# Attention, gated MLP and feed-forward block in one kernel: head 0 loaded ahead and written by the engines, slack for loads on ScalarE, and the output weights converted beside the MoE block of batch 0

## The chip, the cores and the metric

The kernel runs on one core of one Trainium2 chip. The time is the device time of one execution in microseconds; runs of the kernel before gave 665.03, 667.38 and 668.51 us, median 667.38. The engines are PE (TensorE), DVE (VectorE), ACT (ScalarE), POOL (GpSimd) and SP (SyncE, which here only issues DMAs; ACT issues some too).

## The reference

Three stages run one after the other, on 2 batches of 768 positions:

```
# 1 attention: 8 heads of 64; 6 hash bits per row from the sign of q.proj and k.proj
mask   = bucket(q) == bucket(k)
scores = where(mask, q @ k.T / 8, -1e9)
x      = softmax(scores) @ v                       # heads side by side: (2, 768, 512)
# 2 "MoE" block, a gated MLP
u, v   = split(relu(x @ w_in))                     # w_in 512 x 1024, so 512 and 512
gated  = u * (w_spatial @ layernorm(v) + b_spatial)
x      = gated @ w_out                             # 512 x 512
# 3 feed-forward
out    = x + relu(layernorm(x) * g_ln @ w_ch1) @ w_ch2    # 512 -> 2048 -> 512
```

The weights of stages 2 and 3 arrive as float64, seen as pairs of 32-bit words; q, k, v and the result are float32.

## The kernel before, in words

**Precision.** PE multiplies in a reduced float32 form (F32R). To keep accuracy, each operand is kept as a high part (rounded to F32R) and a low part (the rest), and a product is three passes: high by high, high by low, low by high.

**Attention.** Work goes by (batch, head, group g of 384 queries, tile j of 128 queries): 96 tiles, six to a head. `scores` (line 787) makes a 128x768 tile `sc` in PSUM from `qs` and `ks`: a first matmul over 128 rows (high and low parts of one head stacked) and a second over 76 rows, which adds the high parts and 12 indicator rows. The indicator rows make the mask: `mismatch` (line 700) multiplies the raw q and k of a pair of heads by `sides` (signed copies of the projections), and a comparison on DVE makes the tile `m` of them, with rows that add a huge number wherever a bit differs. `masked_max` (line 799) reads `sc` on DVE into `x` and finds the row maximum; `exps` (816) is ACT's exponential; `transposes` (822) turns `x` on PE into `pt`, which ACT and DVE copy to `e`; after six tiles `weighted` (839) multiplies by v into `po`.

**Head pairs.** `pair_load` (670) loads q and k of two heads into 128 partitions (64 each), `pair_split` (682) makes high and low parts, and `passes_of` (723) gathers them with DMAs on SP into `ks` (per head) and `qs` (per group). For the very first head there is a shorter way: `first_load` (748) also loads head 0's k, and its q of group 0, into partitions 64 to 127 of a tile `dup`, and `first_parts` (754) has the engines write `ks` and the `qs` of group 0 directly, the indicator rows too. Group 1 of head 0, and head 1, still come through `pair_split` and SP's DMAs. While the first data arrive, PE runs 16 + 8 transposes of an identity into a tile `warm`.

**Weights.** Each weight of stage 2 is converted once from float64 words, in 4 pieces of 128x512 per matrix: ACT issues the load (`stage_f64`, 561), ACT and DVE work on the words (`words_f64`, 567), POOL joins them (`join_f64`), ACT and POOL split them into high and low. `conversions` (973) lists w_out, then the v half, then the u half of w_in; `CONV_AT` gives the attention tile at which each piece begins (5, 9, ... 57) and `CONV_D` the delays of its four steps. A finished matrix is written whole to DRAM (`kept`, 963), and loaded back by `reload` (994) when a batch needs it. w_out is collected in the tile that later holds the normalized v (`vn`).

**Stages 2 and 3.** `moe1(0)` begins at attention tile 60 and runs interleaved with tiles 60 to 95; `moe1(1)` runs with the first matmuls of stage 3 (`up`, `down`), whose weights `w1` and `w2` are converted in pieces like those above (`f_w`, `f64c_w`, `w1t`, `w2t`), in buffers (`conv1`, two of them) that open when attention ends.

**What sets the order.** No engine's order is the program's. Each call makes a Job; `run` (296) is a list scheduler with modelled durations, which picks on every engine the ready job that is due first; `latest` (397) works back from the end for due times; twelve rounds alternate, the best is kept, and `issue` (472) emits each engine's instructions in that order. A job isn't planned more than `EARLY` = 20 us ahead of its due time, nor more than 60 jobs ahead of PE. `plan.behind` names a job that the next jobs are planned after; it makes no semaphore. On the chip an engine runs its instructions strictly in that order, and waits where data are late; ACT's DMA issues stand in the same order as its arithmetic.

Every instruction of the program is recorded at line 494, where `issue` emits it, so the rows are told apart by tiles.

Of the kernel before, what the change touches and what calls it, by code (L numbers as in the profile page):

```python
# [18 lines left out]
P = 128  # L19
# [150 lines left out]
class Plan:  # L170
# [12 lines left out]
    NEXT = 0.03  # L183
    LAND = {"load": 2.0, "move": 1.5, "store": 1.5}
    RATE = {"load": 300e3, "move": 195e3, "store": 200e3}

    def __init__(self, tc):
        self.tc, self.jobs, self.pools, self.part, self.behind = tc, [], [], 0, None
        for name, key in (("tensor", "PE"), ("vector", "DVE"), ("scalar", "ACT"), ("gpsimd", "POOL"), ("sync", "SP")):
            setattr(self, name, Engine(self, key))  # L190

    def add(self, engine, op, args, kw):
        writes = [kw["out"] if "out" in kw else args[0]]
        rest = [*(args if "out" in kw else args[1:]), *(x for k, x in kw.items() if k not in ("out", "accum_out"))]
        if "accum_out" in kw:
            writes.append(kw["accum_out"])
        reads = [x for x in rest if isinstance(x, View)]
        views = [(x, True) for x in writes if isinstance(x, View)] + [(x, False) for x in reads]
        prev = self.jobs[-1] if self.jobs else None
        if (  # L200
            engine == "PE"
            and prev is not None
            and prev.engine == "PE"
            and prev.part == self.part
            and not prev.closed
            and prev.out is writes[0].base
            and prev.kind == (op, cells(writes[0]), writes[0].rows)
            and len(prev.calls) < (12 if cells(writes[0]) == 384 and op == "matmul" and reads[0].dtype == F32 else self.RUN)
        ):
            job = prev  # L210
        else:
            job = Job(len(self.jobs), engine, self.part)
            self.jobs.append(job)
            if engine == "PE":
                job.out, job.kind = writes[0].base, (op, cells(writes[0]), writes[0].rows)
        if self.behind:
# [15 lines left out]
    def cost(self, engine, op, writes, reads, kw, job):  # L232
# [12 lines left out]
        if engine == "PE":  # L245
            if op == "transpose":
                return (0.109 if isinstance(reads[0], View) else 0.213), 0.165
# [48 lines left out]
    def run(self, late=None):  # L296
# [20 lines left out]
        def opened(j):  # L317
# [182 lines left out]
def attn_moe_kernel(ctx: ExitStack, tc: tile.TileContext, qT, kT, v, proj, w_in, w_spT, b_sp, w_out, g_ln, w1, w2, out):  # L500
# [20 lines left out]
    CONV_AT = (5, 9, 14, 19, 24, 29, 34, 39, 44, 49, 53, 57)  # L521
# [9 lines left out]
    WARM2 = 8  # L531
# [68 lines left out]
    nc.sync.dma_start(out=pj[0:D], in_=proj)  # L600
# [69 lines left out]
    def pair_load(b, r, first=False, which=(("k", kT), ("q", qT))):  # L670

        pr = pairs.setdefault((b, r), {})
        for nm, src in which:
            pr[nm] = ap.tile([P, 2, S], F32R, tag=nm + "2", name=f"{nm}2_{b}_{r}", bufs=1 if nm == "k" else 2)
            if first:
                raw = ap.tile([P, S], F32, tag="x", name=f"{nm}_raw", bufs=XB)
            else:
                raw = pr[nm][:, LOW[nm]].bitcast(F32)
            nc.sync.dma_start(out=raw, in_=src[b, 2 * r : 2 * r + 2].rearrange("h d s -> (h d) s"))
            pr[nm, "raw"] = raw  # L680

    def pair_split(b, r, first=False):

        for nm in "kq":
# [4 lines left out]
            if first:  # L689
                nc.scalar.activation(hi, raw, AF.Copy, scale=scale)  # L690
# [9 lines left out]
    def mismatch(b, r):  # L700


        m = ap.tile([P, GW], F32R, tag="m", name=f"m_{b}_{r}", bufs=2)
        pm = ps_b.tile([P, GW], F32, tag="b", name=f"pm_{b}_{r}")

        for n, (nm, g) in enumerate((("k", 0), ("k", 1), ("q", 0), ("q", 1))):
            raw = pairs[b, r][nm, "raw"]
            nc.tensor.matmul(
                pm[n * QUAD : (n + 1) * QUAD], side[nm], raw[:, g * GW : (g + 1) * GW], start=True, stop=True
            )  # L710
        nc.vector.tensor_scalar(m, pm, above, worth, op0=ALU.is_gt, op1=ALU.mult)
# [36 lines left out]
    def first_load():  # L748
        dup = ap.tile([P, NKT, GW], F32, tag="e", name="dup", bufs=EB)
        nc.sync.dma_start(out=dup[D:P, 0:2], in_=kT[0, 0].rearrange("d (a s) -> d a s", a=2))  # L750
        nc.sync.dma_start(out=dup[D:P, 2], in_=qT[0, 0, :, 0:GW])
        return dup

    def first_parts(dup):
# [3 lines left out]
        qs = ap.tile([P, 2, GW], F32R, tag="qs", name="qs_0_0_0", bufs=QB)  # L758
# [3 lines left out]
        two = pr["q", "raw"][0:D, 0:GW].rearrange("d (o s) -> d o s", o=1).to_broadcast([D, 2, GW])  # L762
        nc.scalar.activation(qs[0:D], two, AF.Copy, scale=-SCALE)
        nc.scalar.activation(qs[D:P, 0], dup[D:P, 2], AF.Copy, scale=-SCALE)
        nc.vector.scalar_tensor_tensor(
            qs[D:P, 0], dup[D:P, 2], -SCALE, qs[D:P, 0].bitcast(F32), op0=ALU.mult, op1=ALU.subtract
        )
        heads[0, 0], groups[0, 0, 0] = {"ks": ks}, {"qs": qs}
        for n, to in enumerate((ks[D:MR, 1, 0:GW], ks[D:MR, 1, GW:S], qs[D:MR, 1])):
            rows = pr["m"][n * QUAD : n * QUAD + NM].bitcast(F32)  # L770
            if n == 1:
                nc.scalar.activation(to, rows, AF.Copy)
            else:
                nc.vector.tensor_copy(to, rows)
# [24 lines left out]
    def masked_max(b, h, g, j):  # L799
# [14 lines left out]
        t["x"], t["nb"] = x, nb  # L814
# [61 lines left out]
    def attn_step(i):  # L876
# [19 lines left out]
        if 0 < n < NT and order[n][3] == 0:  # L896
            group_prep(*order[n][:3])
# [44 lines left out]
    def converted(src, dst, nm, after=None):  # L942
# [12 lines left out]
        def finish():  # L955
            to = dst()
            split_f64(to[:, 0], to[:, 1], d["f"])
            if after:
                after(to)

        return stage, words, join, finish

    def kept(key, shape, to):
        w_split[key] = dram.tile(shape, F32, tag=f"ws_{key}", name=f"ws_{key}")
        nc.scalar.dma_start(out=w_split[key], in_=to.bitcast(F32))
# [7 lines left out]
    def conversions():  # L973

        res = []
        for key, src, at in (("out", w_out, 0), ("v", w_in, HF), ("u", w_in, 0)):
            for k in range(KFT):

                def dst(key=key, k=k):
                    if k == 0:  # L980
                        if key == "out":
                            wp[key] = mp.tile([P, 2, NKT, HF], F32R, tag="vn", name="w_out", bufs=1)
                        else:
                            wp[key] = moe_tile(key, 0)
                    return wp[key][:, :, k : k + 1]

                def after(to, key=key):
                    kept(key, [P, 2, KFT, HF], wp.pop(key)[:, :, :KFT])

                src_k = src[:, k : k + 1, at : at + HF]  # L990
                res.append(converted(src_k, dst, f"{key}_{k}", after if k == KFT - 1 else None))
# [161 lines left out]
    for i in range(-1 - QA, NT + PO + 3):  # L1153
# [212 lines left out]
```

## Time and profile before

| | |
|---|---|
| median of 3 runs | 667.38 us (665.03 to 668.51) |
| the profiled execution | 669.14 us |
| its span, first to last instruction | 666.8 us |
| mean granted PE clock over the span | 0.992 |
| busy: PE / DVE / ACT / POOL | 651.5 / 430.3 / 302.1 / 198.3 us |
| DMA, mean | 126 GB/s |

The span is what the trace covers; the time of an execution holds some 2 us more. "Busy" of PE is modelled: matmuls are pipelined, so back to back they count as busy without a gap. The clock is a share of full speed: 1.00 is 2.4 GHz, 0.50 is 1.2 GHz. In a timeline, the bracket behind an instruction tells how long its engine was idle before it and what ended that; xN is how many like instructions were merged. "PE", "ACT" and so on are the engines' own work; "SPq" and "ACTq" are DMA issues.

### The profile page before, as it was taken

What the parts mean: (1) busy time and instruction counts of PE and PEld (TensorE: products, weight loads), DVE (VectorE), ACT (ScalarE), POOL (GpSimd) and SP (SyncE); (2) the same over time, 40 slices, a digit from 0 to 9 for tenths busy, and PEclk for the clock granted to TensorE, in tenths of its full rate; (3) what the DMA queues carried; (4) which work ended last, traced back from release to release, by engine and by line L of the source; (5) the groups of instructions that cost most, each with busy time, mean ns of one, the idle gap of its engine ahead of it and who ended that gap; (6) DMA issues with size and microseconds to landing.
All of it is one profiled execution on the core that took longest, in us unless ns stands there. A gap on an engine that the chain in (4) does not pass through costs nothing.

```text
span 666.8 us, 9374 instructions
## 1 busy us (share of the span) xinstructions
PE 651.5 (98%) x3376; PEld 510.2 (77%) x3376; DVE 430.3 (65%) x804; ACT 302.1 (45%) x581; POOL 198.3 (30%) x184
## 2 busy tenths in 40 slices
PE   7999999989999999999899999999999999999997
PEld 5776767767777777877688888888888888888886
DVE  5699779998657544443899695788862358622122
ACT  5788877776556545433364343432321133311110
POOL 2234424446325311100324433054450044510000
PEclk8999999999999999999899999999999999999999
DMA  6776775755539442906343441722210222200031
GB/s 167 187 190 168 190 162 154 220 134 179 146 97 336 102 105 71 327 27 227 129 151 121 144 132 47 284 95 87 84 51 1 64 85 87 81 1 16 1 111 63
DMA packets 47413, 83.72 MB, mean 126 GB/s; under 512 B 5676, under 2 KB 32136, under 8 KB 46344
## 3 DMA queue, kind: packets, MB, share of 16 engines
q1 hardware_dynamic: 34104, 53.64, 28.3%
q10 hardware_dynamic: 13264, 29.50, 13.2%
q8 instruction: 27, 0.44, 0.3%
q14 instruction: 18, 0.15, 0.1%
HBM read 51.42 MB, written 12.58 MB: 96 GB/s over the span
## 4 chain that ended last, share of the span: by engine, by line
PE 87%; DVE 7%; DMA 3%; issue 1%; ACT 1%; POOL 0%; SPq 0%; ACTq 0%; DVEq 0%; POOLq 0%
PE pc L494 20%; PE acc L494 20%; PE pv L494 8%; PE po L494 8%; PE sc L494 8%; PE pg L494 8%; PE pt L494 7%; PE py L494 5%; DVE x L494 2%; DMA f_w<-in_w 1%; DVE f64c_u L494 1%; PE pm L494 1%; PE ptr_g L494 1%; PE px_c L494 1%; DMA qs<-m 1%
## 5 line engine op out<-in xcount | busy, mean ns | idle before, releaser
L494 PE MATMUL acc<-w2t,ch 128*128 128x512 f32 x576 | 141.8, 393 | 0.0
L494 PE MATMUL pc<-xh,w1t 128*128 128x512 f32 x576 | 141.8, 394 | 0.0
L494 PEld LDWEIGHTS pc<-xh,w1t 128*128 128x128 f32 x576 | 108.0, 188 | 24.7
L494 PEld LDWEIGHTS acc<-w2t,ch 128*128 128x128 f32 x576 | 108.0, 188 | 24.5
L494 ACT ACTIVATE x<-x,nb 128x768 f32<-128x768 f32 x96 | 89.7, 935 | 29.9 <-DVE x L494 27.9
L494 DVE TENSOR_SCALAR_CACHE_REDUCE x<-sc 128x768 f32<-128x768 f32 x96 | 90.9, 952 | 17.8 <-PE sc L494 12.0
L494 DVE SCALAR_TENSOR_TENSOR ch<-pc,ch 128x512 fp32r<-128x512 f32 x48 | 33.1, 690 | 106.5 <-ACT ch L494 106.4
L494 PE MATMUL sc<-ks,qs 128*128 128x512 f32 (+3 forms) x384 | 94.9, 367 | 6.9 <-DVE x L494 3.6
L494 ACT ACTIVATE ch<-pc 128x512 fp32r<-128x512 f32 x48 | 28.7, 598 | 146.1 <-PE pc L494 146.0
L494 PE MATMUL pt<-ident,x 128*128 128x128 f32 x576 | 82.6, 276 | 0.9 <-DVE m L494 0.6
L494 PEld LDWEIGHTS sc<-ks,qs 128*128 128x128 f32 (+1 forms) x384 | 64.3, 194 | 21.7 <-DVE x L494 5.7
L494 POOL TENSOR_TENSOR f64c_w<-f_w,f64c_w 128x512 f32<-128x512 f32 x32 | 44.6, 1395 | 114.6 <-DVE f64c_w L494 95.0
L494 PEld LDWEIGHTS pt<-ident,x 128*128 128x128 f32 x576 | 68.0, 142 | 13.3 <-ACT e L494 4.1
L494 ACT ACTIVATE e<-pt 128x384 f32<-128x384 f32 x120 | 55.8, 484 | 26.5 <-PE pt L494 25.8
L494 PE MATMUL po<-e,vv 128*64 128x384 f32 x384 | 65.5, 490 | 0.0
L494 DVE COPY e<-pt 128x384 f32<-128x384 f32 x72 | 39.6, 552 | 17.9 <-PE pt L494 17.6
L494 PEld LDWEIGHTS po<-e,vv 128*64 128x64 f32 x384 | 26.2, 137 | 31.3 <-issue 30.1
L494 PE MATMUL pg<-vn,w_sp 128*128 128x512 f32 x180 | 45.0, 399 | 0.0
L494 PE MATMUL pv<-w_u,act_x 128*128 128x512 f32 x144 | 36.3, 400 | 2.3 <-ACT xT L494 2.2
L494 PEld LDWEIGHTS pg<-vn,w_sp 128*128 128x128 f32 x180 | 33.0, 188 | 7.1
L494 DVE TENSOR_SCALAR f64c_w<-f64c_w 128x512 f32<-128x512 f32 x64 | 32.6, 511 | 7.2 <-ACT f64c_w L494 6.5
L494 PE MATMUL pv<-w_v,act_x 128*128 128x512 f32 x144 | 37.1, 406 | 0.0
(132 smaller groups left out, 777.5 us busy)
## 6 DMA issues: line engine op xcount, KB each, us to landing
f_w<-in_w ACTq DMA_DIRECT2D x32, 512.0 KB
ks<-k SPq DMA_DIRECT2D x45, 192.0 KB
qs<-q SPq DMA_DIRECT2D x31, 192.0 KB
wst_sp<-in_w_spT SPq DMA_DIRECT2D x12, 384.0 KB
w_out<-ws_out SPq DMA_DIRECT2D x2, 2048.0 KB
vv<-in_v SPq DMA_DIRECT2D x16, 192.0 KB
ot<-y_dram SPq DMA_DIRECT2D x12, 256.0 KB
qs<-q SPq DMA_DIRECT2D x31, 96.0 KB
```

The costliest lines, as they stand in the source:

```text
L494: getattr(getattr(nc, engine[j.engine]), op)(*map(live, args), **{k: live(x) for k, x in kw.items()})
```

## The change

Four edits. (1) At the start only head 0's halves of k and q are loaded first (64 partitions), then `dup`, now with both groups of q, then head 1's halves. A first `mismatch` works on rows 0 to 63 alone, followed by ten warm transposes (`WARM2`, 8 before); a second one on all rows follows later for head 1. `first_parts` writes the `qs` of both groups, and POOL copies one set of indicator rows. The low and high parts of the pair (`pair_split`) are planned behind the first masked max and behind the first `m`. The raw tiles take a buffer of the ring `e` instead of two of the ring `x`. (2) The planner has a DMA that ACT issues become ready 2.0 us after the instructions that it waits for (`SLACK`). (3) The order of conversions is v, u, out, with other starting tiles; jobs of these steps may be planned as early as they are ready (`soon`). (4) The four pieces of w_out go through the tiles `sp0` and `sp1` and are each stored on their own, high and low part in one DMA each.

```diff
+    SLACK = 2.0
@@ run @@
-            return max(when[i], bulk, late[j] - self.EARLY) if late else max(when[i], bulk)
+            return max(when[i], bulk, late[j] - self.EARLY) if late and not j.soon else max(when[i], bulk)
...
                         t = j.end + self.HOP.get(h.engine, 0.0)
+                        if h.bytes and h.engine == "ACT":
+                            t += self.SLACK
@@ attn_moe_kernel @@
-    CONV_AT = (5, 9, 14, 19, 24, 29, 34, 39, 44, 49, 53, 57)
+    CONV_AT = (5, 11, 18, 24, 31, 37, 44, 50, 58, 62, 66, 70)
-    WARM2 = 8
+    WARM2 = 10
-    nc.sync.dma_start(out=pj[0:D], in_=proj)
+    nc.scalar.dma_start(out=pj[0:D], in_=proj)
@@ pair_load @@
+        if first:
+            raws = ap.tile([P, 3, S], F32, tag="e", name="raws", bufs=EB)
...
+            if first:
+                nc.sync.dma_start(out=raw[0:D], in_=src[b, 0])
@@ pair_split @@
             if first:
+                plan.behind = made
                 nc.scalar.activation(hi, raw, AF.Copy, scale=scale)
...
+                plan.behind = tiles[0, 0, 0, 0]["max"] if first else None
                 nc.vector.scalar_tensor_tensor(lo, raw, scale, hi.bitcast(F32), op0=ALU.mult, op1=ALU.subtract)
@@ mismatch @@
-                pm[n * QUAD : (n + 1) * QUAD], side[nm], raw[:, g * GW : (g + 1) * GW], start=True, stop=True
+                pm[n * QUAD : (n + 1) * QUAD], side[nm][rows], raw[rows, g * GW : (g + 1) * GW], start=True, stop=True
             )
+        if first:
+            plan.behind = plan.jobs[-1]
+            for _ in range(WARM2):
+                nc.tensor.transpose(warm, ident, ident)
+            plan.behind = None
@@ first_load @@
-        nc.sync.dma_start(out=dup[D:P, 2], in_=qT[0, 0, :, 0:GW])
+        for g in range(NG):
+            nc.sync.dma_start(out=dup[D:P, 2 + g], in_=qT[0, 0, :, g * GW : (g + 1) * GW])
+        for nm, src in (("k", kT), ("q", qT)):
+            nc.sync.dma_start(out=pairs[0, 0][nm, "raw"][D:P], in_=src[0, 1])
@@ first_parts: for g in range(NG), group 1 planned behind made @@
+            nc.scalar.activation(qs[0:D], two, AF.Copy, scale=-SCALE)
+            nc.scalar.activation(qs[D:P, 0], dup[D:P, 2 + g], AF.Copy, scale=-SCALE)
+            nc.vector.scalar_tensor_tensor(
+                qs[D:P, 0], dup[D:P, 2 + g], -SCALE, qs[D:P, 0].bitcast(F32), op0=ALU.mult, op1=ALU.subtract
+            )
+            if g == 0:
+                rows(0, ks[D:MR, 1, 0:GW], nc.vector.tensor_copy)
+                rows(1, ks[D:MR, 1, GW:S], by_act)
+            rows(2 + g, qs[D:MR, 1], by_act if g else nc.gpsimd.tensor_copy)
@@ attn_step @@
-        if 0 < n < NT and order[n][3] == 0:
+        if GRP < n < NT and order[n][3] == 0:
@@ conversions @@
-        for key, src, at in (("out", w_out, 0), ("v", w_in, HF), ("u", w_in, 0)):
+        for key, src, at in (("v", w_in, HF), ("u", w_in, 0), ("out", w_out, 0)):
...
+                    if key == "out":
+                        for i in range(2):
+                            nc.scalar.dma_start(out=w_split[key][:, i, k], in_=to[i].bitcast(F32))
@@ the start and the loop @@
-    made = mismatch(0, 0)
+    made = mismatch(0, 0, slice(0, D))
     first_parts(dup)
     plan.behind = made
-    pair_split(0, 0, first=True)
+    mismatch(0, 0)
     plan.behind = None
-    for _ in range(WARM2):
-        nc.tensor.transpose(warm, ident, ident)
...
+        plan.soon = True
         for e in conv_steps.get(i, ()):
             e()
+        plan.soon = False
```

In `masked_max`, the first tile's call is now what calls `pair_split(0, 0, first=True)`.

## Rows read from the trace of the kernel before

**Rows 1.** Windows: length, busy PE PEld DVE ACT POOL, clock, DMA share, GB/s.

```profile
0.00:20.00 20.00, 15.01 (x70) 12.56 (x71) 10.60 (x23) 11.22 (x19) 4.04 (x26) 0.83 0.67 176
20.00:145.00 125.00, 122.50 (x828) 87.54 (x827) 110.25 (x225) 100.50 (x218) 48.15 (x45) 1.00 0.68 176
145.00:310.00 165.00, 163.08 (x934) 124.73 (x932) 93.92 (x192) 84.14 (x167) 49.12 (x43) 1.00 0.50 152
310.00:345.00 35.00, 32.82 (x145) 26.20 (x142) 27.92 (x67) 18.25 (x33) 7.00 (x6) 0.95 0.51 182
345.00:666.80 321.80, 318.13 (x1408) 259.13 (x1407) 187.59 (x300) 87.99 (x146) 89.96 (x65) 1.00 0.25 83
```

**Rows 2.** Timeline of the first 10 us: first uses of the loads.

```profile
3.78 0.84 ACT L494 ACTIVATE ks<-k_raw 64x768 fp32r<-64x768 f32 x1 [1.16 <-DMA k_raw<-in_kT]
...
6.49 0.84 ACT L494 ACTIVATE qs<-q_raw 64x768 fp32r<-64x768 f32 x1 [1.86 <-DMA q_raw<-in_qT]
...
7.36 0.52 ACT L494 ACTIVATE qs<-dup 64x384 fp32r<-64x384 f32 x1
7.47 0.83 POOL L494 TENSOR_SCALAR ks<-dup 64x768 fp32r<-64x768 f32 x1 [4.02 <-DMA dup<-in_kT]
```

**Rows 3.** Timeline of PE and DVE up to the seventh masked max.

```profile
1.45 4.66 PE L494 MATMUL warm<-ident 128*128 128x128 f32 x24 [1.45 <-POOL above L494]
...
6.60 0.84 PE L494 MATMUL pm<-q_raw,sides 128*32 128x384 f32 x4
...
7.55 0.68 DVE L494 TENSOR_SCALAR m<-pm,above,worth 128x384 fp32r<-128x384 f32 x1 [1.94 <-PE pm L494]
8.26 0.56 DVE L494 SCALAR_TENSOR_TENSOR qs<-dup,qs 64x384 fp32r<-64x384 f32 x1
...
9.21 0.35 DVE L494 CAST qs<-m 12x384 fp32r<-12x384 f32 x1
9.60 1.47 DVE L494 SCALAR_TENSOR_TENSOR q<-q_raw,q 128x768 fp32r<-128x768 f32 x1
...
11.86 0.94 DVE L494 TENSOR_SCALAR_CACHE_REDUCE x<-sc 128x768 f32<-128x768 f32 x1
...
22.21 0.96 DVE L494 TENSOR_SCALAR_CACHE_REDUCE x<-sc 128x768 f32<-128x768 f32 x1
```

**Rows 4.** Windows: the stretch of the start at the lower clock.

```profile
12.00:19.00 7.00, 6.14 (x23) 5.62 (x24) 4.18 (x9) 4.52 (x10) 0.00 (x0) 0.51 0.89 199
```

**Rows 5.** Timeline of DVE and PE at a piece of u.

```profile
145.67 1.50 DVE L494 TENSOR_SCALAR f64c_u<-f64c_u 128x512 uint32<-128x512 uint32 x1
...
148.23 0.98 PE L494 MATMUL sc<-ks,qs 128*128 128x512 f32 x4 [1.54 <-DVE x L494]
```

**Rows 6.** Timeline of ACT and PE after the first load of w1, then a window.

```profile
326.95 0.39 ACTq L494 DMA_DIRECT2D f_w<-in_w  x1
327.44 0.60 ACT L494 ACTIVATE xT<-pv 128x512 f32<-128x512 f32 x1 [4.00 <-POOL f64c_w L494]
...
328.09 1.75 PE L494 MATMUL pv<-w_u,act_x 128*128 128x512 f32 x6 [2.18 <-ACT xT L494]
...
329.00:333.00 4.00, 4.00 (x13) 3.11 (x12) 3.06 (x7) 1.37 (x4) 1.30 (x1) 0.57 0.24 82
```

**Rows 7.** Instructions of the tile f64c_out: DVE's five of a piece, ns min/median/max.

```profile
L494 DVE TENSOR_SCALAR f64c_out<-f64c_out x8: 411/428/1125, 30.2 to 60.6; 128x512 f32<-128x512 f32 x4, 128x512 uint32<-128x512 uint32 x4
...
L494 DVE SCALAR_TENSOR_TENSOR f_out<-f_out,f64c_out x4: 681/694/699, 34.2 to 64.7; 128x512 uint32<-128x512 uint32 x4
L494 DVE TENSOR_SCALAR f64c_out<-f_out x4: 425/426/427, 37.0 to 67.6; 128x512 uint32<-128x512 uint32 x4
L494 DVE SCALAR_TENSOR_TENSOR f64c_out<-f_out,f64c_out x4: 686/754/1658, 39.9 to 68.5; 128x512 f32<-128x512 uint32 x4
```

**Rows 8.** Instructions of the tile w_out: its first use and its reload.

```profile
L494 PE MATMUL py<-w_out,act_g x144: 387/392/505, 244.3 to 419.4; 128*128 128x512 f32 x144
...
L494 SPq DMA_DIRECT2D w_out<-ws_out x2: 339/376/414, 208.5 to 340.5; - x2
```

More of the change, by code (lines that the diff above doesn't have):

```diff
@@ L246, in cost @@
             if op == "transpose":
-                return (0.109 if isinstance(reads[0], View) else 0.213), 0.165
+                return (0.109 if isinstance(reads[0], View) or self.behind else 0.213), 0.165
             if reads[0].dtype == F32:
@@ L697, in pair_split, with mismatch @@
             else:
+                plan.behind = tiles[0, 0, 0, 0]["max"] if first else None
                 nc.vector.scalar_tensor_tensor(lo, raw, scale, hi.bitcast(F32), op0=ALU.mult, op1=ALU.subtract)
-    def mismatch(b, r):
+                plan.behind = None
+    def mismatch(b, r, rows=slice(0, P)):
+        first = rows.stop < P
         m = ap.tile([P, GW], F32R, tag="m", name=f"m_{b}_{r}", bufs=2)
@@ L761, in first_parts, with rows, by_act @@
         split_hi(ks[D:P, 0].rearrange("d (a s) -> d a s", a=2), dup[D:P, 0:2])
[L762 to L774, printed above, removed]
+        heads[0, 0] = {"ks": ks}
+        def rows(n, to, e):
+            e(to, pr["m"][n * QUAD : n * QUAD + NM].bitcast(F32))
+        def by_act(to, src):
+            nc.scalar.activation(to, src, AF.Copy)
+        for g in range(NG):
+            plan.behind = made if g else None
+            qs = ap.tile([P, 2, GW], F32R, tag="qs", name=f"qs_0_0_{g * GW}", bufs=QB)
+            two = pr["q", "raw"][0:D, g * GW : (g + 1) * GW].rearrange("d (o s) -> d o s", o=1).to_broadcast([D, 2, GW])
+            nc.scalar.activation(qs[0:D], two, AF.Copy, scale=-SCALE)
[3 more added lines that the diff above has]
+            )
+            groups[0, 0, g] = {"qs": qs}
+            if g == 0:
+                rows(0, ks[D:MR, 1, 0:GW], nc.vector.tensor_copy)
+                rows(1, ks[D:MR, 1, GW:S], by_act)
+            rows(2 + g, qs[D:MR, 1], by_act if g else nc.gpsimd.tensor_copy)
+        plan.behind = None
     def head_prep(b, h):
@@ L813, in masked_max @@
         )
-        t["x"], t["nb"] = x, nb
+        t["x"], t["nb"], t["max"] = x, nb, plan.jobs[-1]
+        if (b, h, g, j) == (0, 0, 0, 0):
+            pair_split(0, 0, first=True)
     def exps(b, h, g, j):
@@ L956, in finish @@
             to = dst()
[L957 to L959 removed]
+            split_f64(to[0], to[1], d["f"].rearrange("p a n -> p (a n)"))
+            after(to)
         return stage, words, join, finish
[L963 to L965 removed]
     def moe_tile(key, b):
@@ L975, in conversions, with after @@
         res = []
-        for key, src, at in (("out", w_out, 0), ("v", w_in, HF), ("u", w_in, 0)):
+        for key, src, at in (("v", w_in, HF), ("u", w_in, 0), ("out", w_out, 0)):
+            w_split[key] = dram.tile([P, 2, KFT, HF], F32, tag=f"ws_{key}", name=f"ws_{key}")
             for k in range(KFT):
                 def dst(key=key, k=k):
-                    if k == 0:
[L981 to L988, printed above, removed]
+                    if key == "out":
+                        parts = [
+                            mp.tile([P, NKT * P], F32R, tag=f"sp{i}", name=f"w_out_{k}_{i}", bufs=2 - i) for i in range(2)
+                        ]
+                        return [x[:, :HF] for x in parts]
+                    if k == 0:
+                        wp[key] = moe_tile(key, 0)
+                    return [wp[key][:, i, k] for i in range(2)]
+                def after(to, key=key, k=k):
+                    if key == "out":
+                        for i in range(2):
+                            nc.scalar.dma_start(out=w_split[key][:, i, k], in_=to[i].bitcast(F32))
+                    elif k == KFT - 1:
+                        nc.scalar.dma_start(out=w_split[key], in_=wp.pop(key).bitcast(F32))
                 src_k = src[:, k : k + 1, at : at + HF]
-                res.append(converted(src_k, dst, f"{key}_{k}", after if k == KFT - 1 else None))
+                res.append(converted(src_k, dst, f"{key}_{k}", after))
         return res
```

10 lines of the change are left out of this document (6 added, 4 removed).

## The prediction

> **What bounds the kernel now.** I read the windows by stage first. In the five stages PE is busy 15.01, 122.50, 163.08, 32.82 and 318.13 us, 651.54 of the 666.8 us span [rows 1]. From 345 us on it runs without a gap that a change ahead of it could use; what is to be had lies in 0 to 20 (4.99 us idle, clock 0.83), in 20 to 150, and in 310 to 345 (2.18 us idle, clock 0.95). So the kernel is bound by TensorE, and a change pays only by what it takes out of PE's gaps and out of stretches at the lower clock.
>
> Then the timeline of the first 25 us. The 384 KB of k are first used at 3.78, those of q at 6.49, the 192 KB of dup at 7.47 [rows 2]. PE is through with warming and mismatch at 7.44, the indicator rows are done at 9.56, and then DVE does the low parts of q and k for head 1 from 9.60 on (1.47 for q's) before the first masked max at 11.86 [rows 3], 2.3 us in all. PE is almost empty meanwhile, and from 12 to 19 its granted clock is 0.51, the 1.2 GHz level, over 6.14 us of busy time [rows 4]: about 6.14/2 = 3.1 us are lost there. The seventh masked max comes at 22.21 [rows 3]; after it PE is full.
>
> Last, the waits inside the body. At 148.23 PE waits 1.54 us for a masked max that stands on DVE behind words of a u piece, one of them stretched to 1.50 [rows 5]. At 328.09 PE waits 2.18 us for ACT's xT, which itself stood 4.00 us until the POOL join of the first w1 piece [rows 6]: the instruction ahead of it on ACT is the issue of the third f_w load, which needs a buffer that this join releases. After that gap the clock is 0.57 over 329 to 333, which costs 4 x 0.43 = 1.7 us [rows 6].
>
> **The start.** Removed: half of the bytes ahead of the first mismatch, one small load on SP (pj goes to ACT's queue, ahead of the table load and the first activation, where ACT waits for data anyway), three DMAs for group 1 of head 0, and the two low parts ahead of the first max. Added: a second mismatch (4 matmuls, and 0.68 on DVE for m), engine-written parts for group 1 (ACT 0.84 + 0.52 + 0.52, DVE 0.56 by the like rows [rows 2, 3]), two warm transposes, the copy of one set of rows moved to POOL. Loads go up by three (q's second group, and two second halves) and SP's early list shrinks by one in all.
>
> Landing: 1056 KB were in by 7.47 and 384 by 3.78, so 672 KB took 3.69 us, 182 KB per us [rows 2]. At this pace 192 KB of k, 192 of q, 192 of dup k and 96 of dup q are in at 2.7, 3.8, 4.8 and 5.4 us. Sixteen of the 24 warm transposes take at least 16/24 of 4.66 and end between 4.6 and 4.9 [rows 3]. The mismatch can so run at 4.9 instead of 6.6, m is done near 6.5 instead of 8.2, and behind it DVE has 0.56 + 0.35 in place of 0.56 + 0.35 + 0.35: the operands are whole at about 7.5 instead of 9.56, 2.0 us earlier. POOL's copy of 12x384 has no row before; DVE's like copy took 0.35 [rows 3] and POOL's 64x768 0.83 [rows 2], so 0.35 to 0.83, and I take 0.5; it runs beside DVE's copy. Behind it on POOL waits only the split for the next pair. The new order behind `made` and behind the first max binds only the planner; it is no semaphore.
>
> First max: with the low parts behind it, two score tiles after 7.5 give 8.2 instead of 11.86, 3.7 us. Part of that is paid back. From the first to the seventh max the engines need: DVE about 1.3 a tile (0.94 for a max, its read-out, an eviction in every second tile), 7.9 for six, plus 2.3 + 0.68 + 0.56 = 3.5, so the seventh comes near 8.2 + 7.9 + 3.5 - 1 (what fits ahead of the first) = 18.6 by DVE. By ACT, which has some 1.8 us a tile (before, 22.21 - 11.86 = 10.4 us for six) and 1.9 us more, it is near 19.5 to 20. PE would need less at the 2.4 GHz level. I take 19.5 for 22.21: **2.7 us gained**. Ends: 4.0 (no idle left on DVE), and -0.5 (head 1's seven DMAs, issued only after the low parts, hold its first scores, and the clock falls as before). The ten warm transposes stand between mismatch and scores, where PE idles otherwise; if the scores were ready sooner they would cost at most 10/24 of 4.66 = 1.9.
>
> Here a rule of the Trainium skill speaks against the change: "DMA: Bandwidth & Descriptors", section "Rules for kernel authors", says of two transfers to disjoint halves of the partitions that they serialize on the same engines, and to use one of 128 partitions. This trace shows 199 GB/s in 12 to 19, where most copies have 64 partitions [rows 4], no worse than the pace above. By the rule the landing term would be lost; it is rival 3.
>
> **The conversions.** One piece costs DVE 2 x 0.428 + 0.694 + 0.426 + 0.754 = 2.7 us [rows 7]. Four of twelve leave tiles 5 to 57 and go to 58 to 73; those left stand 6 to 7 tiles apart instead of 4 to 5, and u is done some seven tiles before the MoE block begins, not in it. DVE is busy 110.25 of 125 us in 20 to 145 [rows 1]; 8 x 2.7 in place of some 11 x 2.7 takes it to about 102. PE's idle there is 2.50 [rows 1], and the wait at 148 is 1.54 [rows 5]: 4.0 at most; as the order is made anew and waits for rows by DMA stay, I take half, **2.0 gained**; ends 4.0 and -2.0 (new waits in their place, as many as half of the old).
>
> Beside the MoE block DVE has 93.92 busy of 165 [rows 1], so 4 x 2.7 = 11 us fit, less the u pieces that leave. ACT issues eight stores of 256 KB in place of one of 2 MB, ahead of nothing urgent: the reload of the output weights is issued at 208.5 and used first at 244.3 [rows 8]. I charge **0.5 lost**; ends 0 and 6.2 (four waits as long as the 1.54 of rows 5).
>
> **The slack.** The planner thinks that the third f_w load can be issued at once after ACT's work on the second piece; the chip held it until the join. Two microseconds later in the plan, the xT that PE needs can come ahead of it. If the 4.00 us on ACT fall to 2.0, PE's 2.18 nearly vanish, and the clock with them: at best 2.18 + 1.7 = 3.9. The buffer's release is not earlier, and the pieces behind come later by as much; w1 and w2 feed a stage where PE is full, so late is only what makes this stage's first pc wait. I take half again, **2.0 gained**; ends 3.9 and -1.0.
>
> **Sum.** The profiled execution took 669.14 (span 666.8 and 2.3 around it). 669.14 - 2.7 - 2.0 + 0.5 - 2.0 = 662.9. It stands 1.8 above the median of the runs, 667.38, so the forecast for the median is 661.2.
>
> **Rivals.**
> 1. *Head 1 becomes the wait.* At the start the first max is early, but the DMAs of head 1 or a clock of 0.5 again give most back: the start gains 0.5, not 2.7. For it: seven DMAs, issued one after the other, begin only behind the low parts. Against it: PE is emptier for less time than before 12 us. 661.2 + 2.2 = 663.4.
> 2. *Only the start counts.* The plan is made anew; the gaps at 148 and 328 go and others like them come. 667.4 - 2.7 = 664.7. For it: each wait hangs on how plan and chip differ by one or two us. This is also the case that slack and weights don't do what they are meant to.
> 3. *Halves land no sooner.* A 64-partition load takes as long as the 128-partition one in its place; q is in at 6.49 as now [rows 2]. Then 2.0 of the start's 2.7 is lost: 663.2.
> 4. *The output weights crowd the MoE block.* DVE is nearly full before 160; four pieces of 2.7 us that go as early as they can stand ahead of masked maxes as in rows 5. Four waits of 1.54 are 6.2, and two falls of the clock as in rows 6 are 3.4: 9.6. With the start's 2.7 that is 667.4 + 6.9 = 674.3. It decides from where PE's new waits from 140 to 200 us exceed some 6 us: then all that is gained elsewhere is gone. Against it: these pieces are due late, and the planner ranks by due time.
>
> **How the numbers follow.** Chances: forecast 0.50, rival 1 0.17, rival 2 0.18, rival 3 0.05, rival 4 0.10. The forecast's own range is 657 to 665.5 (its ends do not fall together); with the rivals 656 to 668.5, leaving out rival 4 and the best tenth. A measurement of this kernel can tell some 0.5% (3.3 us) from no change, so faster is under 664.0 and slower over 670.7. Faster: 0.48 of the forecast, 0.09 of rival 1, 0.05 of 2, 0.03 of 3: 0.65. Slower: 0.10, nearly all rival 4. The rest, 0.25, is no change.
>
> **What would show it.** Start: first masked max near 8.2, the seventh near 19.5, a clock of 1.0 in 12 to 19. If q's first use is still at 6.5, rival 3. If the seventh max is past 21.5, rival 1, and the wait before head 1's first score names it. Conversions: no PE wait on DVE near u's last piece. MoE block: PE busy over 163 of 165 us, else rival 4. Slack: ACT's wait on the first join under 2 us, and no clock of 0.5 at 330. The prediction is wrong if PE's gaps past 20 us sum to what they do now, or if its stage from 345 on is no longer full.

## The result and the profile after

The changed kernel takes 661.34 us (median of 5 runs, 660.59 to 663.74) against 667.38 of the kernel before (5 runs, 665.03 to 668.51): ratio 0.9903, 95% interval 0.9882 to 0.9925. 661.2 was forecast. Its profiled execution took 661.69 us, span 659.6, mean granted clock 1.00: 7.45 us less than the 669.14 of before.

First the windows by stage of the changed kernel, against [rows 1], and below them the stretch of [rows 4].

```profile
0.00:20.00 20.00, 16.08 (x93) 11.84 (x94) 12.52 (x28) 14.96 (x26) 5.37 (x27) 1.00 0.72 184
20.00:145.00 125.00, 122.02 (x826) 87.67 (x824) 102.86 (x214) 95.45 (x212) 44.90 (x43) 1.00 0.69 182
145.00:310.00 165.00, 164.25 (x937) 126.34 (x938) 99.05 (x204) 87.00 (x173) 52.23 (x45) 1.00 0.52 154
310.00:345.00 35.00, 35.00 (x160) 28.23 (x159) 31.14 (x70) 19.37 (x35) 11.94 (x10) 1.00 0.52 179
345.00:659.60 314.60, 310.83 (x1375) 252.62 (x1373) 184.55 (x291) 85.98 (x141) 80.43 (x61) 1.00 0.25 81
...
12.00:19.00 7.00, 6.43 (x41) 5.03 (x39) 6.06 (x12) 6.93 (x16) 0.00 (x0) 1.00 0.79 205
```

The clock of the start is 1.00 instead of 0.83, that of 310 to 345 is 1.00 instead of 0.95, and there PE has no gap left. From 20 to 145 DVE lost 7.4 us of work, and PE, with 122.02 for 122.50, gained nothing by it.

A window begins at a fixed time, and the work in it shifts. So I also took the start of the same matmul in both traces. The changed kernel is 1.83 us ahead near 143 us (the first scores of the eleventh head), 4.00 at 317.5 (the last `pv` of `w_u` ahead of the old gap), 6.36 behind the gap and 7.30 at 453.6, where it stays. By stages: start 1.8, attention to 143 nothing, from there to the gap 2.2, the gap and the clock behind it 3.3. PE's idle time from 20 to 345 us falls from 6.60 to 3.73 us, and its stage from 345 on is as full as it was (3.77 us idle, 3.67 before).

The start, in the timeline of the changed kernel (compare [rows 2, 3]):

```profile
4.29 0.84 ACT L498 ACTIVATE qs<-raws 64x768 fp32r<-64x768 f32 x1 [1.05 <-DMA raws<-in_qT]
...
5.36 0.85 PE L498 MATMUL pm<-raws,sides 64*32 64x384 f32 x8 [0.44 <-DMA raws<-in_kT]
...
6.12 0.95 DVE L498 TENSOR_TENSOR ks<-raws,ks 64x768 fp32r<-64x768 f32 x1 [1.26 <-ACT ks L498]
...
6.15 1.61 POOL L498 TENSOR_SCALAR ks<-dup 64x768 fp32r<-64x768 f32 x1 [2.71 <-DMA dup<-in_kT]
...
6.99 0.67 DVE L498 TENSOR_SCALAR m<-pm,above,worth 128x384 fp32r<-128x384 f32 x1
...
7.62 1.67 PE L498 MATMUL pm<-raws,sides 128*32 128x384 f32 x8 [0.17 <-DMA raws<-in_kT]
...
7.83 0.78 POOL L498 CAST qs<-m 12x384 fp32r<-12x384 f32 x1
8.28 0.55 DVE L498 CAST ks<-m 12x384 fp32r<-12x384 f32 x1
...
9.22 1.69 PE L498 MATMUL sc<-ks,qs 128*128 128x512 f32 x8
...
10.62 0.95 DVE L498 TENSOR_SCALAR_CACHE_REDUCE x<-sc 128x768 f32<-128x768 f32 x1
...
20.45 0.96 DVE L498 TENSOR_SCALAR_CACHE_REDUCE x<-sc 128x768 f32<-128x768 f32 x1 [0.79 <-PE sc L498]
```

The operands are whole at 8.83 (8.28 + 0.55), not at 7.5, and the first scores start at 9.22, because the second mismatch, which waits for head 1's halves, stands ahead of them on PE. The first max comes 1.24 us earlier, the seventh 1.76.

The body, in the same timeline; the last four rows answer [rows 6].

```profile
81.22 0.74 PE L498 MATMUL sc<-ks,qs 76*128 76x512 f32 x3 [1.64 <-DMA qs<-m]
...
145.75 0.98 PE L498 MATMUL sc<-ks,qs 128*128 128x512 f32 x4 [0.89 <-DVE x L498]
...
321.09 0.58 ACT L498 ACTIVATE xT<-pv 128x512 f32<-128x512 f32 x1
...
321.73 1.64 PE L498 MATMUL pv<-w_u,act_x 128*128 128x512 f32 x6
...
323.18 0.39 ACTq L498 DMA_DIRECT2D f_w<-in_w  x1
...
323.61 0.63 ACT L498 ACTIVATE w1t<-f64c_w 128x512 fp32r<-128x512 f32 x1 [1.94 <-POOL f64c_w L498]
```

The wait of [rows 5] shrank to 0.89, a new one of 1.64 for a DMA stands at 81, and at the old gap xT now runs ahead of the third f_w load, which still waits for its buffer but holds up nobody.

### The profile page after: what moved, and what is told of

Read it like the earlier page. It is cut to its first block, busy times and chain, and to the rows that moved or that the text cites. A ratio compares the mean times of both kernels' runs of the same rounds, so it can differ in the third digit from the quotient of the medians.

```text
span 659.6 us, 9420 instructions
## 1 busy us (share of the span) xinstructions
PE 648.2 (98%) x3386; PEld 506.7 (77%) x3386; DVE 430.1 (65%) x805; ACT 302.8 (46%) x584; POOL 194.9 (30%) x185
## 4 chain that ended last, share of the span: by engine, by line
PE 90%; DVE 4%; DMA 2%; ACT 2%; SPq 1%; issue 1%; POOL 0%; DVEq 0%; ACTq 0%
PE pc L498 20%; PE acc L498 20%; PE pv L498 10%; PE po L498 9%; PE sc L498 8%; PE pg L498 8%; PE pt L498 8%; PE py L498 5%; DMA qs<-m 2%; DVE x L498 1%; ACT x L498 1%; PE px_c L498 1%; PE ptr_g L498 1%; SPq L498 1%; DVE f64c_u L498 1%
## 5 line engine op out<-in xcount | busy, mean ns | idle before, releaser
L498 PE MATMUL sc<-ks,qs 128*128 128x512 f32 (+3 forms) x384 | 92.8, 362 | 4.6 <-DMA qs<-m 2.2
L498 PE MATMUL pt<-ident,x 128*128 128x128 f32 x576 | 81.0, 274 | 1.0 <-ACT x L498 0.8
L498 PEld LDWEIGHTS pt<-ident,x 128*128 128x128 f32 x576 | 66.3, 141 | 13.2 <-issue 4.9
L498 DVE TENSOR_SCALAR f64c_w<-f64c_w 128x512 f32<-128x512 f32 (+1 forms) x64 | 37.3, 587 | 14.1 <-ACT f64c_w L498 13.1
L498 ACT ACTIVATE f64c_w<-f_w 128x512 f32<-128x512 f32 x32 | 21.2, 668 | 34.7 <-DMA f_w<-in_w 33.5
L498 PE MATMUL py<-w_out,act_g 128*128 128x512 f32 x144 | 36.0, 396 | 0.0
```

The lines of the kernel that those rows point to most:

```text
L498: getattr(getattr(nc, engine[j.engine]), op)(*map(live, args), **{k: live(x) for k, x in kw.items()})
```

## The experiments

"Before" took 667.5 to 667.6 us (medians) beside the first eleven, 665.86 beside the last. Ratios are to that, with their 95% intervals; they rest on all runs and differ by up to 0.14% from the quotients of the medians. Matched matmuls compare one profiled execution of each kernel.

**The gap at 328.** Is it one place in ACT's order? Kernel before, only this instruction moved, every other order the same (in `issue`; `load` is ACT's third f_w load, `relu` the xT that PE waits for at 328):

```diff
...
+        order.insert(max(load, relu), order.pop(min(load, relu)))
```

> The kernel before, with one thing changed: on ACT, the issue of the third f_w load (first words of the second w1 piece) comes behind the xT that PE waited for at 328 us, instead of ahead of it. All other instructions of all engines are in the same order. Theory (that load, standing for a buffer, held ACT and by it PE): PE's wait of 2.18 and the half clock after it both go, 3.3 to 3.9 us, so 663.5 to 664. Rival (xT was held by the join itself or by something else that ends as late): the wait stays within 0.5 us and the time is 667.

665.33 us, ratio 0.9969 (0.9948 to 0.9989). The timeline of this kernel:

```profile
324.03 0.60 ACT L500 ACTIVATE xT<-pv 128x512 f32<-128x512 f32 x1 [1.42 <-PE pv L500]
...
325.22 1.55 PE L500 MATMUL pv<-w_u,act_x 128*128 128x512 f32 x6
...
326.27 0.39 ACTq L500 DMA_DIRECT2D f_w<-in_w  x1
```

And its window over the stretch that ends [rows 6]:

```profile
329.00:333.00 4.00, 3.98 (x20) 2.85 (x18) 4.00 (x9) 3.13 (x7) 0.77 (x1) 1.00 0.06 20
```

The wait is gone and the clock is 1.00 instead of 0.57. At matched matmuls this kernel is 0.52 us ahead of before up to the gap and 3.64 behind it: one instruction's place costs 3.1 us, wait and clock together. The medians differ by 2.2 us, less than the 3.3 to 3.9 expected; the profiled execution of before, with 669.14, lies 1.8 above its median. Second, the kernel before with the slack alone:

```diff
+    SLACK = 2.0
...
+                        if h.bytes and h.engine == "ACT":
+                            t += self.SLACK
```

> The kernel before with the 2.0 us of slack for ACT's loads alone (no change of start or conversions). Theory: the order at the third f_w load changes as in the swap, 3.3 us gained there, and up to 1 us either way in the body: 663 to 665. Rival (any new plan does as well, slack as such is worth nothing): the gap may go, but the body loses or gains at random, 662 to 668.

663.62 us, 0.9927 (0.9902 to 0.9951): 3.9 us less. The gap is gone here too; a new wait of 2.3 us for `qs<-q` appears near 135.

**The start.** Alone: the changed kernel with the slack at 0 and the old conversions.

```diff
-    SLACK = 2.0
+    SLACK = 0.0
...
-    CONV_AT = (5, 11, 18, 24, 31, 37, 44, 50, 58, 62, 66, 70)
+    CONV_AT = (5, 9, 14, 19, 24, 29, 34, 39, 44, 49, 53, 57)
...
-        for key, src, at in (("v", w_in, HF), ("u", w_in, 0), ("out", w_out, 0)):
+        for key, src, at in (("out", w_out, 0), ("v", w_in, HF), ("u", w_in, 0)):
...
-        plan.soon = True
```

> The kernel before with the new start alone (slack 0, old conversions). Theory: the start is worth the 1.8 us by which the seventh masked max is earlier in the changed kernel, so 665.5 with the gap at 328 us still there. Rival (the start also shapes what follows): under 664 or over 667.

664.39 us, 0.9944 (0.9923 to 0.9964): 3.1 us less. The seventh max comes at 20.21, the clock of the start is 1.00, and the old gap stays: 1.86 us, here at 322.9. Behind it the clock is 1.00 (322 to 334), where before had 0.57, so the lower clock doesn't always come with this gap. Next, the changed kernel with the second mismatch behind the second tile's scores:

```diff
         tiles[b, h, g, j] = {"sc": sc}
+        if (b, h, g, j) == (0, 0, 0, 1):
+            plan.behind = plan.jobs[-1]
+            mismatch(0, 0)
+            plan.behind = None
...
-    plan.behind = made
-    mismatch(0, 0)
-    plan.behind = None
```

> The changed kernel with the second mismatch (for head 1) planned behind the scores of tile 1 instead of ahead of the first scores. Theory that it stands 0.4 us in the way of the first scores, because it waits for the second half of q: first masked max at 10.2 instead of 10.62, the seventh up to 0.4 earlier (20.0 to 20.5), time 660.9 to 661.3. Rival, that head 1's own chain (rows, copies by DMA, low parts) sets the seventh max: first max earlier, the seventh at 20.5 or later, time 661.3 to 663.

666.92 us, 0.999 (0.9971 to 1.001), a miss for both. Its first and seventh masked max, in the timeline:

```profile
10.27 0.96 DVE L498 TENSOR_SCALAR_CACHE_REDUCE x<-sc 128x768 f32<-128x768 f32 x1 [1.68 <-PE sc L498]
...
21.48 0.96 DVE L498 TENSOR_SCALAR_CACHE_REDUCE x<-sc 128x768 f32<-128x768 f32 x1 [1.29 <-PE sc L498]
```

And three of its waits from 20 to 160 us (engine, line, what it waited for, us in total, times, longest):

```profile
PE sc L498 <- DMA ks<-k: 2.4, 1, 2.4
PE sc L498 <- DMA qs<-m: 2.3, 1, 2.3
...
PE sc L498 <- DMA qs<-q: 1.1, 1, 1.1
```

The first max is 0.35 earlier, nearly as computed, and the seventh 1.03 later: its group waits for head 1's DMAs (the third wait, at 20.4), which now start later. The other two waits stand at 149.3 and 83.5, far from the edit, since the planner made the whole order anew. At matched matmuls this kernel is 1.65 us later than the changed one at 26 us, and 6.1 later near 143. Last, whole loads instead of halves:

```diff
-                nc.sync.dma_start(out=raw[0:D], in_=src[b, 0])
+                nc.sync.dma_start(out=raw, in_=src[b, 0:2].rearrange("h d s -> (h d) s"))
...
-        for nm, src in (("k", kT), ("q", qT)):
-            nc.sync.dma_start(out=pairs[0, 0][nm, "raw"][D:P], in_=src[0, 1])
```

> The changed kernel with the whole k and q of the first pair loaded (128 partitions, 384 KB each) instead of head 0's half first and head 1's half after dup. Theory that a half lands hardly sooner than the whole: q's first use moves from 4.29 by less than 1 us, k's as well, and the first masked max stays within 0.7 us of 10.62; time 661 to 662.3. Rival, that halves save what their bytes take (384 KB less ahead of dup at 182 KB per us, 2.1 us): first max at 12.5 or later, time 663 or more.

670.43 us, 1.005 (1.0025 to 1.0076). The time again holds waits of the body (7.3 us for DMAs from 20 to 160), so only its start bears on the question, in the timeline:

```profile
3.84 0.84 ACT L498 ACTIVATE ks<-raws 64x768 fp32r<-64x768 f32 x1 [0.61 <-DMA raws<-in_kT]
...
6.43 0.84 ACT L498 ACTIVATE qs<-raws 64x768 fp32r<-64x768 f32 x1 [1.75 <-DMA raws<-in_qT]
...
11.48 0.95 DVE L498 TENSOR_SCALAR_CACHE_REDUCE x<-sc 128x768 f32<-128x768 f32 x1
```

The first whole load is used at 3.84, earlier than the first half at 4.29. The second whole is in at 6.43, the second half at 5.36 at the latest. So halves bring the first max forward by 0.86 us: more than the one theory had, far less than the 2 us of the other.

**The parts together.** Start and slack: the kernel with the start alone, and

```diff
-    SLACK = 0.0
+    SLACK = 2.0
```

> The changed kernel with the old conversions (out, v, u at the old tiles, one 2 MB store each, no early rank): start and slack together, without the third part. Theory that start and slack carry the whole gain: alone they gave 3.1 us (664.39) and 3.9 us (663.62), so together about 660.5, from 659 to 662, no slower than the changed kernel's 661.3; the 2 MB store of v stays in the MoE stage and no PE wait for an operand's load near 79 us. Rival, as predicted, that the conversions carry 1.5 us of it (2.0 gained, 0.5 lost): 662.8 or more.

663.73 us, 0.994 (0.9922 to 0.9958). The sum theory misses by 3 us, 3.1 and 3.9 don't add: at matched matmuls this kernel is only 0.15 us ahead of before near 145 (it waits 3.2 us for DMAs from 20 to 160, before 1.0) and gains 2.35 at the gap. The time lies where the rival had it, so on top of these two parts the conversions bring 2.4 us in the changed plan. Whether they do so of themselves, the next runs tell. The changed kernel without slack:

```diff
-    SLACK = 2.0
+    SLACK = 0.0
```

> The changed kernel with slack 0. If slack is what closes the gap at 328 us, the gap comes back: 661.3 + 3.5 = 665. Rival (the new plan closes it by itself, slack isn't needed): 661 to 662, and ACT's order there has xT ahead of the load all the same.

674.05 us, 1.0095 (1.0065 to 1.0124): slower than before, by 12.7 us slower than the changed kernel. Not by the gap: PE idles 0.64 us in all from 310 to 345, and in the timeline xT stands ahead of the third f_w load without the slack too, as the rival had it:

```profile
326.90 0.58 ACT L498 ACTIVATE xT<-pv 128x512 f32<-128x512 f32 x1
...
329.72 0.39 ACTq L498 DMA_DIRECT2D f_w<-in_w  x1
```

Its waits from 20 to 160:

```profile
PE sc L498 <- DMA ks<-k: 3.0, 1, 3.0
PE sc L498 <- DMA qs<-q: 1.6, 1, 1.6
PE pm L498 <- DMA k<-in_kT: 1.5, 1, 1.5
```

And its timeline of 96 to 115:

```profile
99.23 0.41 ACTq L498 DMA_DIRECT2D ws_v<-w_v  x1
...
109.19 0.52 PE L498 MATMUL pm<-k,sides 128*32 128x384 f32 x2 [1.47 <-DMA k<-in_kT]
...
112.07 1.15 PE L498 MATMUL sc<-ks,qs 128*128 128x512 f32 x2 [1.55 <-DMA qs<-q]
```

Two of the three waits follow the 2 MB store of v's finished weights. Before, ACT issued it at 198.9, in the MoE block; in the changed kernel it goes at 74.8, since v is now converted first and may be planned as soon as it is ready, 6.4 us ahead of the new wait at 81. Then the conversions alone, on the kernel before:

```diff
-    CONV_AT = (5, 9, 14, 19, 24, 29, 34, 39, 44, 49, 53, 57)
+    CONV_AT = (5, 11, 18, 24, 31, 37, 44, 50, 58, 62, 66, 70)
...
-        for key, src, at in (("out", w_out, 0), ("v", w_in, HF), ("u", w_in, 0)):
+        for key, src, at in (("v", w_in, HF), ("u", w_in, 0), ("out", w_out, 0)):
...
+        plan.soon = True
```

> The kernel before with the new conversions alone (v, u, out at the new tiles, the early rank; no slack, old start). Theory that this conversion order puts v's 2 MB store on ACT in the attention stage, beside the next heads' loads, and that without the slack this costs as it did with the new start (674.05 against 664.39, 9.7 us): about 677, from 673 to 681, with PE waits for DMA of 1.5 us and more between 30 and 115 us. Rival, that only the plan of start and conversions together was bad: 667.5 or less, as the conversions were predicted to gain 1.5.

674.13 us, 1.0088 (1.0055 to 1.0122): 6.6 us slower than before, where the theory had 673 to 681. By themselves the conversions bring nothing but the end of the gap at 328: PE is busy 34.70 of the 35 us from 310 to 345, without the slack.

**The store.** Four kernels move v's store in ACT's order and nothing else on any engine, three of them so (in `issue`, when the order is made; `store` finds ACT's first store to a tensor):

```diff
...
+        first = store("ws_out")
+        order.insert(first - 1, order.pop(store("ws_v")))
```

In the conversions alone:

> The conversions alone (as in the sixth experiment, 674.13) with the same one instruction moved, v's store from 77.4 us to ahead of the first store of the output weights. Theory: the wait of 4.4 us for qs at 85 to 90 goes, with the fall of the clock (0.95 in 80 to 145) behind it, 8.7 us of slack in 80 to 100 down to some 1.5: 667.5, from 666 to 670. Rival, that the new order is late there without the store: the wait stays over 2 us and the time over 672.

668.01 us, 1.0007 (0.9986 to 1.0028): 6.1 us given back. Windows of the conversions alone around the store:

```profile
76.00:86.00 10.00, 6.00 (x47) 4.70 (x45) 7.00 (x14) 6.68 (x14) 3.19 (x3) 1.00 0.91 323
86.00:94.00 8.00, 7.63 (x28) 3.53 (x28) 4.01 (x8) 1.03 (x2) 1.30 (x1) 0.58 0.42 91
```

In its chain of waits from 70 to 92 (start, us, what) the longest piece is

```profile
77.71 8.57 DMA qs<-q
```

The same windows with the store late:

```profile
76.00:86.00 10.00, 10.00 (x72) 7.07 (x73) 9.55 (x20) 7.81 (x17) 3.64 (x3) 1.00 0.77 192
86.00:94.00 8.00, 7.47 (x53) 5.88 (x50) 6.14 (x11) 5.43 (x12) 2.58 (x2) 1.00 0.50 149
```

With the early store the DMAs move 323 GB/s instead of 192, a copy of q into `qs`, issued by SP, is 8.57 us under way, PE idles 4 us, and its clock is 0.58 afterwards. The Trainium skill says in "DMA: Bandwidth & Descriptors", section "Issuing engines are not separate DMA queues", that DMAs share the same 16 DMA engines and interleave whoever issues them; the trace agrees, ACT's store against SP's copies. In the changed kernel without slack:

> The changed kernel without the slack (as in the third experiment, 674.05) with the same one instruction moved, v's store from 99.2 us to ahead of the first store of the output weights. Theory: the waits of 1.5 us for k and 1.6 us for qs at 109 and 112 go with what follows them (5.3 us of slack in 100 to 120 down to 1.5), the wait of 3.0 us for ks at 35 stays, as it lies ahead of the store: 670, from 668.5 to 671.5. Rival, that both waits stay, since the loads are late by their own order: 673 or more.

667.80 us, 1.0009 (0.999 to 1.0028): 6.25 us given back, more than expected. Both waits behind the store are gone; that at 35, ahead of it, is still 2.4. In the changed kernel itself:

> The changed kernel with one instruction moved in ScalarE's order: the 2 MB store of v's weights goes from 74.8 us to just ahead of the first store of the output weights (about 190 us); every other instruction keeps its place. Theory that this store, beside the next heads' loads, causes the wait of 1.6 us for qs at 79: that wait falls under 0.4 and the time to 659.8, from 659 to 660.8. Rival, that the loads' order on the queue makes the wait by itself: the wait stays near 1.6 and the time at 661.3. Second rival, that the store is missed in the MoE stage instead, beside u's 2 MB store and eight stores of 256 KB: waits of 1 us and more from 185 to 240, 662 or more.

663.90 us, 0.9939 (0.9912 to 0.9965): no faster. The wait at 81 is gone, and this kernel is 2.97 us ahead of the changed one near 143. Of that 0.98 comes at 60.6, ahead of the store's old place, where the order of the two is the same, and isn't the store's; 2.0 comes from 81 on. But v's store now goes at 152.7, and the second rival's wait comes, earlier than it was expected, in the timeline:

```profile
149.44 0.36 ACTq L507 DMA_DIRECT2D ws_u<-w_u  x1
150.82 0.33 SPq L507 DMA_DIRECT2D k<-in_kT  x1
152.74 0.33 ACTq L507 DMA_DIRECT2D ws_v<-w_v  x1
...
165.65 0.33 ACTq L507 DMA_DIRECT2D ws_out<-w_out  x1
166.02 0.60 ACT L507 ACTIVATE xT<-pv 128x512 f32<-128x512 f32 x1 [3.27 <-DMA k<-in_kT]
...
166.77 0.52 PE L507 MATMUL pz<-ident,zw 128*128 128x128 f32 x3 [2.25 <-ACT xT L507]
```

Two stores of 2 MB go 3.3 us apart; ACT stands still from 162.75 (162.56 + 0.19 for its last read-out) to its next store at 165.65, xT is queued behind that, and PE waits 2.25. Of the 2.97, 0.46 are left near 178. So the last run puts v's store where the changed kernel moves next to nothing, behind the last store of the output weights:

```diff
-        order.insert(first - 1, order.pop(store("ws_v")))
+        order.insert(stores("ws_out")[-1], order.pop(stores("ws_v")[0]))
```

> The changed kernel with v's 2 MB store moved on ScalarE to just behind the last store of the output weights (about 195 to 198 us), ahead of the stretch from 205 to 212 in which the changed kernel moves next to nothing; nothing else moves. Theory: the ninth experiment's gain in the attention stage (2.97 us at 143) stays, and its new wait of 2.3 us at 165, from two 2 MB stores 3.3 us apart, is gone: 658.5, from 657.5 to 660.5, no PE wait of over 1 us from 20 to 250 us. Rival, that a 2 MB store stands in the way wherever it goes (here of the reload of the output weights at 214 and of the loads of heads at 197 to 205): a wait of 1.5 us and more from 195 to 250, 660.5 to 663.

658.83 us (658.37 to 659.74, 6 runs), 0.988 (0.9852 to 0.9908). Its windows:

```profile
20.00:145.00 125.00, 123.18 (x836) 89.13 (x835) 105.57 (x220) 97.72 (x216) 45.58 (x44) 1.00 0.66 170
145.00:310.00 165.00, 165.00 (x940) 126.84 (x939) 97.90 (x203) 85.81 (x171) 51.66 (x45) 1.00 0.56 170
```

And all of PE's waits from 20 to 345 us:

```profile
PE sc L506 <- DVE x L506: 0.9, 1, 0.9
PE sc L506 <- DMA qs<-m: 0.4, 1, 0.4
PE pt L506 <- ACT x L506: 0.3, 1, 0.3
```

PE is full from 145 on. At matched matmuls it is level with the changed kernel at 60.6 and 2.0 us ahead from 93 to the end. The intervals of the two ratios still overlap; its slowest run, 659.74, lies below the changed kernel's fastest of five, 660.59. It is the fastest kernel of this study.

All kernels, from 20 to 160 us (140 us), by when v's store is issued:

| kernel | store, us | PE waits for DMAs | PE busy | ratio |
|---|---|---|---|---|
| before | 198.9 | 1.0 | 135.92 | 1 |
| xT ahead of the load | 198.3 | 0.4 | 136.94 | 0.9969 |
| slack alone | 204.5 | 2.3 | 136.52 | 0.9927 |
| start alone | 196.1 | 1.0 | 137.78 | 0.9944 |
| start and slack | 200.2 | 3.2 | 135.94 | 0.994 |
| changed | 74.8 | 2.2 | 136.27 | 0.9903 |
| changed, no slack | 99.2 | 6.1 | 132.22 | 1.0095 |
| conversions alone | 77.4 | 4.4 | 131.73 | 1.0088 |
| second mismatch later | 76.3 | 6.3 | 132.46 | 0.999 |
| whole loads | 74.5 | 7.3 | 131.30 | 1.005 |
| changed, store late | 152.7 | 0.6 | 138.64 | 0.9939 |
| conversions, store late | 165.2 | 5.2 | 133.66 | 1.0007 |
| no slack, store late | 154.7 | 2.9 | 136.55 | 1.0009 |
| changed, store in the gap | 196.1 | 0.4 | 138.18 | 0.988 |

Of five kernels with the store before 100 us four have PE busy 131.3 to 132.5; the changed kernel is the one that got through. With the store late all but one lie at 135.9 or more; the exception, with 133.66, has a wait of 4.1 us for `qs<-m` near 150, ahead of its store. It has another 2 MB store ahead of it: u's, which goes at 267.1 in the kernel before and at 134.6 to 152.4 wherever the conversions are new. Here it goes at 134.64, and the load of 512 KB that ACT issues next is 13.83 us under way. The kernels with the second mismatch later and with whole loads, too, have a wait for an operand's DMA (2.4 and 1.7 us) some 10 us behind u's store; the changed kernel, with u's store at 152.4, has none. No run moved u's store alone, so its price is not shown.

## Why the prediction was right, and where it was not

The forecast of 661.2 met 661.34 with gains in the terms that err both ways: 2.7 + 2.0 - 0.5 + 2.0 = 6.2 was worked out, and the stages show 1.8 + 0 + 2.2 + 3.3 = 7.3 of the 7.45. That the total fits so closely is luck. The terms are read from profiled executions, which came 1.2 us further apart than forecast; but the profiled execution stands 0.35 above its median after the change, where the prediction took the 1.8 of before for both, so the medians differ by 6.0.

**The start**, 2.7 forecast, 1.8 found. The step that failed is the landing "at this pace": 192 KB were put at 2.7 us and were used at 4.29. Bytes alone don't set it: a whole load of 384 KB was in at 3.84 in the run with whole loads. Rival 3 is right for the first load and not for the pair: q was not "in at 6.49 as now", and splitting, with the halves that are needed later behind, gained 0.86 us of first max. The rule that it leaned on ("Rules for kernel authors" of "DMA: Bandwidth & Descriptors" in the Trainium skill: two loads to disjoint halves serialize) agrees with these rows: the two halves, 384 KB together, were in after 4.29 and by 5.36, one whole load of as much at 3.84. The second error is the second mismatch ahead of the scores, 0.39 us of PE (9.22 - 8.83), which the prediction had listed and given no time. The copies took 0.55 and 0.78, near the upper end for POOL's and above the 0.35 taken for DVE's. The clock of 1.00 in 12 to 19 came as forecast. Rival 1 did not happen: what was won by the first max (1.24) was still there at the seventh (1.76).

**The conversions**, 2.0 forecast to 145, nothing found. DVE's side was right: "about 102" was 102.86. But the prediction moved the steps without one of their DMAs: it looked at the "eight stores of 256 KB in place of one of 2 MB" and not at v's own 2 MB store, which goes with its last piece from the MoE block into the stage where the heads' loads have no room. "Nothing" is a gain less this store: in the last run, the same order with the store in the gap, the lead over before near 143 is 3.87 us in place of 1.83. That this gain of 2.0 beyond the start's 1.8 is the conversions' own is not shown: the conversions alone, store late, are 0.47 behind before at 140, and the changed kernel without slack, store late, is 1.29 ahead, less than the start's 1.8. That store costs 6.1 and 6.25 us in two kernels where it was moved alone, and some 2 in the changed one. Rival 4 came near in kind, crowding by what the conversions bring, but had the wrong stage and the wrong resource: DVE near 160, where it was the DMA engines near 80. It put the crowding at 9.6, and the conversions alone were 6.6 slower.

**Beside the MoE block**, 0.5 lost forecast, 2.2 gained found. The wait of [rows 5], which the prediction had counted with the conversions, fell to 0.89, and PE's idle time in this stage from 1.92 to 0.75, 1.2 of the 2.2. The other us is not tied to a row; a matched point moves by as much when the order of tiles and weights around it changes.

**The slack**, 2.0 forecast, 3.3 found. The mechanism was right and I halved it for no reason that a row gave: the full 2.18 + 1.7 was to be had. Moving the one instruction gave 3.1 at the gap. ACT's wait for the join is 1.94 and now hurts nobody. But in the changed kernel it isn't the slack that closes the gap: without it xT stands ahead of the load as well, and the new conversions alone leave 0.30 us of idle time there. Either part is enough, the slack with the old conversions or the new conversions without it, so the 3.3 belongs to no single term. What the slack is worth in the changed kernel lies elsewhere, as it moves every DMA that ACT issues in the plan. With v's store late in both, the changed kernel takes 667.80 without and 663.90 with it. At matched matmuls they are 7.0 and 7.9 us ahead of before at 350, and 2.95 and 7.66 at 453. PE idles 2.3 us from 345 to 460 without it and not at all with it, in the stage from which the prediction expected nothing; the rest of these 4 us is not tied to a row.

**Rival 2** (the plan is made anew and other gaps come) was right about the mechanism and named the true uncertainty: start and slack, 3.1 and 3.9 alone, give 3.8 together. What stays open is how much of each part's figure is its own and how much the luck of a new plan; moving single instructions, as with xT and the store, is what separated the two here.

## What to carry to other kernels

When a step moves to another stage, list the transfers that it ends with, and look at what the stage's DMA engines carry: a 2 MB store that nobody waits for cost 6 us in two kernels and 2 in a third where small copies were due, and PE no wait where the DMAs idled. Where a planner makes the whole order anew, test a cause by moving one instruction in the finished order; a changed parameter also moves everything else: two edits of the first 10 us of the changed kernel cost 5.6 and 9.1 us, most of it past 70 us. And a DMA issue that must wait for its buffer is an instruction like any other on its engine: put the arithmetic that PE needs ahead of it.

## What the runs showed of the hardware that I had not expected

- A load of 192 KB into 64 partitions, issued at 0.73, was first used at 4.29; one of 384 KB into 128 partitions, issued at the same 0.73 in the run with whole loads, at 3.84.
- POOL's 64x768 `ks<-dup` took 1.61 us beside DVE's subtraction of two operands in SBUF, begun 0.03 us earlier and 0.95 long, and 0.83 without [rows 2]; the excess, 0.78, is nearly DVE's 0.95. The Trainium skill has in "SBUF — State Buffer", section "SBUF: two separate sides", a port pair that one of these two engines locks for a whole instruction, DVE when it has two SBUF inputs; the trace agrees.
- With two stores of 2 MB under way ACT stood 2.9 us ahead of issuing a store of 256 KB whose data it had written itself 3.8 us before (the changed kernel with the store late). The profile names the landing of a load issued by SP as what let it go on; that store doesn't read this load's data, so what it waited for stays open.
